# Block-causal attention and FFN on one core: softmax normalisation of the first two batches on POOL instead of DVE

## The chip, the cores and the metric

The kernel runs on one core of one Trainium2 chip. The metric is the device time of one execution in microseconds (us). Five engines work side by side, each in the order of its own instruction stream: TensorE (PE, with its weight loads PEld), VectorE (DVE), ScalarE (ACT), GpSimd (POOL) and SyncE (SP), which issues the DMA transfers here.

## What is computed

Eight batches of eight heads, 576 positions, head size 64, in fp32. The attention is causal by blocks of 64 positions; its output, the heads side by side, goes through a feed-forward network (FFN) of 512 to 2048 to 512 with a clipped-square activation.

```python
scores = scale * np.matmul(q, k.transpose(0, 1, 3, 2))
scores = np.where(block_i >= block_j, scores, -1e9)
attn = np.exp(scores - np.max(scores, axis=-1, keepdims=True))
attn = attn / (np.sum(attn, axis=-1, keepdims=True) + 1e-09)
x = np.matmul(attn, v)            # -> [4608, 512], heads side by side
h = x @ w_in
g = np.where(h >= 1, h, np.where(h <= -1, 0.0, (h + 1) ** 2 / 4))
out = g @ w_out
```

## The kernel before, in words

**Pairs and steps.** Two heads of one batch form a `Pair`; there are 32, four to a batch. `attention_steps` (L552) cuts each pair into eight steps. Each step gives PE some new work of the pair and some finishing work of an earlier step: `scores` makes one group of score tiles, and `turn` transposes the probabilities of the group scored two steps earlier. Per pair there are six groups (two heads times 128+256, 384 and 512 columns; the first holds two tiles) and one last tile of 576 columns for both heads (`scores_last`).

**One group.** PE multiplies q by k into PSUM (L371, L374), DVE takes the row maximum (L394), ACT exponentiates into the SBUF tile `pr` and sums the row into `sm` (L398), DVE adds a small constant and inverts the sum (L380, L381), and then DVE multiplies `pr` in place by this [128, 1] column (L404; L430 for the last tile). These products are the "norms" below: eight of L404 and one of L430 per pair, 3136 columns in all. After its norm, `pr` is read by PE's transposes (L443 in batches 0 to 2; from batch 3, `HOP`, a DMA copies it first and L441 reads the copy). There are three `pr` buffers.

**Weights.** The inputs of the FFN matmuls are split in a high and a low part (fp32r). `convert` (L151) makes these parts of the FFN weights in 64 pieces of 128x256, in a ring over the engines: ACT scales the two halves of the 64-bit input words (L164, L165), DVE clips, shifts and merges bits (L166, L169, L172), POOL adds integers (L178), ACT rounds to the high part (L180) and POOL subtracts for the low part (L182). The pieces are handed out over the attention steps and lie in the first quarter of the run.

**FFN.** From step 36 (`START`, in the fifth pair) each attention step also brings a half step of the FFN: 12 matmuls of L626, the activation (ACT L635, DVE L636 and L639, ACT L640, POOL L641 for the low part `gl`), and the 12 matmuls of L650 and L655. After the last pair the FFN runs alone.

**Order.** The steps are written in this order, and a scheduler of the framework then sets each engine's stream, so that the place of an instruction can differ by some rows from the written order. Also on POOL: the subtraction that splits k (L302), the split of v (L317, from batch 1) and the low part of x (L546). In batch 0 (`plain`) v and the probabilities stay unsplit.

Of the kernel before, what the change touches and what calls it, by code (L numbers as in the profile page):

```python
# [23 lines left out]
def block_attn_then_ffn(  # L24
# [9 lines left out]
    nc = tc.nc  # L34
# [42 lines left out]
    def work_bank(name):  # L77

        banks["n"] += 1
        if banks["free"] and banks["n"] % 2:  # L80
            return ps_o.tile([P, 512], F32, tag="po", name=name)
        return ps_w.tile([P, 512], F32, tag="work", name=name)
# [138 lines left out]
    def as_float32r(src):  # L221

        moved = []
        for c0 in range(0, src.shape[1], TCH):
            n = min(TCH, src.shape[1] - c0)
            pool, tag = ((conv, "bits"), (conv2, "work"))[c0 > 0]
            dst = pool.tile([P, TCH], F32R, tag=tag, name="prr")
            nc.sync.dma_start(dst[:, :n].bitcast(F32), src[:, c0 : c0 + n])
            moved.append(dst)
        return moved  # L230


    class Pair:
# [4 lines left out]
        def __init__(self, b, hp):  # L238
            self.b, self.hp = b, hp

            self.plain = b == 0
            self.first = b == 0 and hp == 0

            self.hop = b >= HOP
            self.pr, self.nat = {}, {}
# [137 lines left out]
        def scores(self, j, g):  # L383
            tiles = self.GROUPS[g]
            m = len(tiles)
            ps = work_bank("ps_s")
            pr = att3.tile([P, S], F32, tag="pr", name="pr")
            nm = small.tile([P, 2], F32, tag="nm", name="nm")
            sm = small.tile([P, 2], F32, tag="sm", name="sm")
            cols = [slice(at, at + (t + 1) * P) for t, at in tiles]  # L390
            for (t, _), cs in zip(tiles, cols):
                self.product(ps[:, cs], j, t * P, 0, (t + 1) * P, True, True)
            for i, cs in enumerate(cols):
                nc.vector.tensor_reduce(  # L394
                    out=nm[:, i : i + 1], in_=ps[:, cs], axis=AX.X, op=ALU.max, negate=True
                )
            for i, cs in enumerate(cols):
                nc.scalar.activation(  # L398
                    pr[:, cs], ps[:, cs], AF.Exp, bias=nm[:, i : i + 1], scale=1.0,
                    accum_out=sm[:, i : i + 1],  # L400
                )
            self.inverse(sm[:, :m])
            for i, cs in enumerate(cols):
                nc.vector.tensor_scalar_mul(pr[:, cs], pr[:, cs], sm[:, i : i + 1])  # L404
            self.pr[j, g] = as_float32r(pr[:, : cols[-1].stop]) if self.hop else [pr]

        def scores_last(self):

            half = S // 2
            pr = att3.tile([P, S], F32, tag="pr", name="pr")  # L410
            nm = small.tile([P, 3], F32, tag="nm", name="nm")
            sm = small.tile([P, 3], F32, tag="sm", name="sm")
            banks = []
            for i in range(2):
                ps = work_bank("ps_s")
                for j in range(2):
                    self.product(ps[:, :half], j, SM, i * half, half, j == 0, j == 1)
                nc.vector.tensor_reduce(
                    out=nm[:, i : i + 1], in_=ps[:, :half], axis=AX.X, op=ALU.max, negate=True
                )  # L420
                banks.append(ps)
            nc.vector.tensor_tensor(out=nm[:, 2:3], in0=nm[:, 0:1], in1=nm[:, 1:2], op=ALU.min)
            for i in range(2):
                nc.scalar.activation(
                    pr[:, i * half : (i + 1) * half], banks[i][:, :half], AF.Exp,
                    bias=nm[:, 2:3], scale=1.0, accum_out=sm[:, i : i + 1],
                )
            nc.vector.tensor_tensor(out=sm[:, 2:3], in0=sm[:, 0:1], in1=sm[:, 1:2], op=ALU.add)
            self.inverse(sm[:, 2:3])
            nc.vector.tensor_scalar_mul(pr, pr, sm[:, 2:3])  # L430
            self.pr["last"] = as_float32r(pr) if self.hop else [pr]

        def split(self, ps, hi, lo=None):
# [307 lines left out]
```

## Time and profile before

| | |
|---|---|
| median of 3 runs | 1284.82 us (1283.32 to 1285.23) |
| the profiled execution's own time | 1285.23 us |
| its span, first to last instruction | 1283.5 us |
| mean granted TensorE clock | 0.983 |
| busy share PE / DVE / ACT / POOL | 94% / 69% / 60% / 37% |
| first norms of pairs 0, 4, 7, 8 (start) | 18.1, 108.0, 245.7, 285.2 us |
| last weight piece on DVE (start of the last L172) | 253.5 us |

The profile's first part gives the busy time of each engine, the second cuts the span in 40 slices of 32 us and prints the busy share of each in tenths. Tables by stretch list, for each engine, busy time and the number of instructions in brackets. Groups list line, engine, operation, output and input, shapes, count, busy time, mean ns of one, and the engine's idle time ahead of them with what ended it. The chain of waits follows the work that ended last backwards, from each instruction to what released it. A line number is that of the kernel before; the changed kernel is two lines longer from `Pair` on.

### The profile page before, as it was taken

How to read it: one execution, taken by the hardware profiler on the slowest of the kernel's cores; microseconds unless marked ns; L12 is line 12 of the kernel's file. 1: busy time of each engine (PE TensorE's matmuls, PEld its weight loads, DVE VectorE, ACT ScalarE, POOL GpSimd, SP SyncE). 2: the span in 40 equal slices, each digit the busy share in tenths (PEclk: the TensorE clock that was granted, in tenths of full speed). 3: DMA queues.
4: the chain of work that ended last, by engine and by line, in shares of the span. 5: the costliest groups of instructions: out<-in, count | busy, mean ns of one | idle time of the engine just before them, and what ended most of it. 6: DMA issues, size and time to landing. Idle time of an engine off the chain costs nothing.

```text
span 1283.5 us, 20410 instructions
## 1 busy us (share of the span) xinstructions
PE 1207.2 (94%) x6496; PEld 1018.7 (79%) x6496; DVE 888.4 (69%) x2204; ACT 766.3 (60%) x1855; POOL 472.2 (37%) x466
## 2 busy tenths in 40 slices
PE   5877787899999999999999999999999999999998
PEld 4666665688888888888888888888888888888886
DVE  8998999877677777677777777777777767322222
ACT  6878676666666666666666666666666655322222
POOL 3545766633333333333333333333333332222222
PEclk9889999999999999999999999999999999999999
DMA  5656555434333545555444644464545443333432
GB/s 152 175 151 180 170 186 177 145 125 140 97 106 111 189 143 153 160 159 178 147 155 154 187 137 152 153 189 148 159 146 186 156 142 120 115 99 99 132 99 99
DMA packets 136812, 188.44 MB, mean 147 GB/s; under 512 B 61040, under 2 KB 87664, under 8 KB 136704
## 3 DMA queue, kind: packets, MB, share of 16 engines
q1 hardware_dynamic: 136704, 187.13, 47.2%
q8 instruction: 52, 0.85, 0.3%
q14 instruction: 56, 0.46, 0.1%
HBM read 120.59 MB, written 17.83 MB: 108 GB/s over the span
## 4 chain that ended last, share of the span: by engine, by line
PE 70%; DVE 13%; ACT 8%; issue 4%; DMA 2%; POOL 1%; SPq 1%; ACTq 0%; POOLq 0%; DVEq 0%
PE ph L626 26%; PE po L650 16%; PE po L655 8%; PE ps_av L480 7%; PE ps_s L371 3%; PE ps_s L374 3%; ACT pr L398 3%; PE ps_t L441 3%; PE ps_qk L327 2%; DVE pr L404 2%; ACT qb L331 2%; DVE nm L394 2%; DVE work L169 1%; PE ps_t L443 1%; DVE work L172 1%
## 5 line engine op out<-in xcount | busy, mean ns | idle before, releaser
L641 POOL TENSOR_TENSOR gl<-t,gh 128x512 fp32r<-128x512 f32 x144 | 187.2, 1300 | 577.5 <-ACT gh L640 310.8
L650 PE MATMUL po<-wo,gh 128*128 128x512 f32 x1152 | 299.7, 403 | 0.1
L650 PEld LDWEIGHTS po<-wo,gh 128*128 128x128 f32 x1152 | 210.6, 190 | 40.3 <-ACT gh L640 0.6
L626 PE MATMUL ph<-xh,wih 128*128 128x512 f32 x576 | 238.2, 414 | 1.7 <-DVE t L639 1.7
L636 DVE SCALAR_TENSOR_TENSOR t<-t 128x512 f32<-128x512 f32 x144 | 112.9, 784 | 183.1 <-ACT t L635 181.0
L626 PE MATMUL ph<-xl,wih 128*128 128x512 f32 x576 | 227.4, 395 | 1.1 <-DVE xl L516 1.1
L626 PE MATMUL ph<-xh,wil 128*128 128x512 f32 x576 | 227.9, 396 | 0.0
L635 ACT ACTIVATE t<-ph 128x512 f32<-128x512 f32 x144 | 86.0, 597 | 155.2 <-PE ph L626 155.2
L398 ACT ACTIVATE pr<-ps_s,nm 128x128 f32<-128x128 f32 (+3 forms) x256 | 134.2, 529 | 63.1 <-DVE nm L394 62.8
L655 PE MATMUL po<-wo,gl 128*128 128x512 f32 x576 | 155.4, 391 | 0.0
L394 DVE TENSOR_REDUCE nm<-ps_s 128x1 f32<-128x128 f32 (+3 forms) x256 | 123.6, 485 | 45.2 <-PE ps_s L374 43.6
L371 PE MATMUL ps_s<-ka,qa 68*128 68x288 f32 (+4 forms) x384 | 123.6, 336 | 20.5 <-ACT pr L398 12.8
L640 ACT CAST gh<-t 128x512 fp32r<-128x512 f32 x144 | 90.0, 625 | 84.6 <-DVE t L639 83.0
L626 PEld LDWEIGHTS ph<-xh,wil 128*128 128x128 f32 x576 | 109.4, 190 | 24.5
L434 ACT CAST pb<-ps_t 128x512 fp32r<-128x512 f32 (+1 forms) x140 | 77.5, 553 | 84.8 <-PE ps_t L441 65.5
L317 POOL TENSOR_TENSOR vsr<-vn,vsr 128x256 fp32r<-128x256 f32 (+1 forms) x112 | 82.9, 750 | 119.9 <-ACT vsr L316 119.9
L655 PEld LDWEIGHTS po<-wo,gl 128*128 128x128 f32 x576 | 108.4, 188 | 23.4
L626 PEld LDWEIGHTS ph<-xl,wih 128*128 128x128 f32 x576 | 109.9, 191 | 20.4 <-DVE xl L516 1.4
L626 PEld LDWEIGHTS ph<-xh,wih 128*128 128x128 f32 x576 | 109.4, 190 | 20.3 <-DVE t L639 2.0
L374 PE MATMUL ps_s<-kb,qb 128*128 128x288 f32 (+4 forms) x384 | 121.8, 323 | 0.0
L436 DVE TENSOR_TENSOR pb<-ps_t,pb 128x512 fp32r<-128x512 f32 (+1 forms) x140 | 88.1, 629 | 40.5 <-ACT pb L434 40.5
L404 DVE TENSOR_SCALAR pr<-pr,sm 128x128 f32<-128x128 f32 (+3 forms) x256 | 110.3, 451 | 3.6
(95 smaller groups left out, 2039.1 us busy)
## 6 DMA issues: line engine op xcount, KB each, us to landing
wo<-wo_split SPq DMA_DIRECT2D x144, 512.0 KB, 3.4
prr<-pr SPq DMA_DIRECT2D x80, 192.0 KB, 2.6
prr<-pr SPq DMA_DIRECT2D x60, 256.0 KB, 2.4
out_dram<-ob SPq DMA_DIRECT2D x36, 256.0 KB, 4.0
qn<-in_q_dram SPq DMA_DIRECT2D x32, 256.0 KB, 2.9
kn<-in_k_dram SPq DMA_DIRECT2D x32, 256.0 KB, 3.0
bits<-in_moe_w_in_dram SPq DMA_DIRECT2D x32, 256.0 KB, 3.1
bits<-in_moe_w_out_dram SPq DMA_DIRECT2D x32, 256.0 KB, 3.1
```

The source lines that it names most:

```text
L371: nc.tensor.matmul(ps, qa[:KA, j, c0 : c0 + P], ka[:KA, j, k0 : k0 + n], start=first, stop=False)
L374: nc.tensor.matmul(ps, qb[:, j, c0 : c0 + P], kb[:, j, k0 : k0 + n], start=False, stop=last)
L394: nc.vector.tensor_reduce(out=nm[:, i : i + 1], in_=ps[:, cs], axis=AX.X, op=ALU.max, negate=True)
L398: nc.scalar.activation(pr[:, cs], ps[:, cs], AF.Exp, bias=nm[:, i : i + 1], scale=1.0, accum_out=sm[:, i : i + 1],)
L404: nc.vector.tensor_scalar_mul(pr[:, cs], pr[:, cs], sm[:, i : i + 1])
L480: nc.tensor.matmul(ps[:, lo_col:], vt, x, start=first and i == 0 and m == 0, stop=last and i == len(parts) - 1 and m == len(mov) - 1,)
L626: nc.tensor.matmul(ph, w[:, cc, fs], x[:, cc, xs], start=(cc == 0 and i == 0), stop=(cc == NCC - 1 and i == 2),)
L636: nc.vector.scalar_tensor_tensor(out=t_, in0=t_, scalar=1.0, in1=t_, op0=ALU.min, op1=ALU.mult)
L640: nc.scalar.copy(gh, t_)
L641: nc.gpsimd.tensor_tensor(out=gl, in0=t_, in1=gh.bitcast(F32), op=ALU.subtract)
L650: nc.tensor.matmul(po[tt], gh[:, ts_], wo[:, w, :], start=(fc == 0 and w == 0), stop=False)
L655: nc.tensor.matmul(po[tt], gl[:, ts_], wo[:, 0, :], start=False, stop=fc == NFC - 1)
```

## The change

A field of `Pair` names the engine of the norms: POOL for batches 0 and 1 (the first eight pairs), DVE for all others. All 72 norms of these eight pairs (64 of L404 and 8 of L430) change engine; nothing else is written differently.

```diff
             self.plain = b == 0
+
+            self.norm = nc.gpsimd if b < 2 else nc.vector
             self.first = b == 0 and hp == 0
...
             self.inverse(sm[:, :m])
             for i, cs in enumerate(cols):
-                nc.vector.tensor_scalar_mul(pr[:, cs], pr[:, cs], sm[:, i : i + 1])
+                self.norm.tensor_scalar_mul(pr[:, cs], pr[:, cs], sm[:, i : i + 1])
...
             self.inverse(sm[:, 2:3])
-            nc.vector.tensor_scalar_mul(pr, pr, sm[:, 2:3])
+            self.norm.tensor_scalar_mul(pr, pr, sm[:, 2:3])
```

The scheduler places the moved instructions and shifts some neighbours. On DVE, in the second pair (batch 0), between the inversion of the first group's sums and the casts that follow, before the change:

```order
L381 RECIPROCAL sm<-sm 128x2
L291 TENSOR_SCALAR qs<-qn 128x64
L172 SCALAR_TENSOR_TENSOR work<-work 128x256
L404 TENSOR_SCALAR pr<-pr,sm 128x128
L404 TENSOR_SCALAR pr<-pr,sm 128x256
L380 TENSOR_SCALAR sm<-sm 128x1
L351 CAST qa<-ps_qk 64x2x64
L381 RECIPROCAL sm<-sm 128x1
L166 TENSOR_SCALAR work<-work 128x256
L404 TENSOR_SCALAR pr<-pr,sm 128x384
L351 CAST ka<-ps_qk 64x2x64
L169 TENSOR_SCALAR work<-work 128x256
```

The same place on DVE after the change (L383 is the former L381, L294 the former L292, L303 the former L301):

```order
L383 RECIPROCAL sm<-sm 128x2
L293 TENSOR_SCALAR qs<-qn 128x64
L172 SCALAR_TENSOR_TENSOR work<-work 128x256
L294 SCALAR_TENSOR_TENSOR qs<-qn,qs 128x9x64
L382 TENSOR_SCALAR sm<-sm 128x1
L353 CAST qa<-ps_qk 64x2x64
L383 RECIPROCAL sm<-sm 128x1
L166 TENSOR_SCALAR work<-work 128x256
L303 CAST ks<-kn 128x8x64
L353 CAST ka<-ps_qk 64x2x64
L169 TENSOR_SCALAR work<-work 128x256
L303 CAST ks<-kn 128x64
```

The norms are gone, and the splits of the next pair's q and k move up into their places.

On POOL in the fifth pair, the first of batch 1, around the split of the next pair's k (L302), before the change:

```order
L182 TENSOR_TENSOR ws<-work,ws 128x256
L178 TENSOR_TENSOR work<-work,bits 128x256
L182 TENSOR_TENSOR wil<-work,wih 128x256
L178 TENSOR_TENSOR work<-work,bits 128x256
L302 TENSOR_TENSOR ks<-kn,ks 128x9x64
L182 TENSOR_TENSOR wil<-work,wih 128x256
L178 TENSOR_TENSOR work<-work,bits 128x256
L641 TENSOR_TENSOR gl<-t,gh 128x512
```

The same place on POOL after the change (L304 is the former L302, L406 and L432 the norms, L643 the former L641):

```order
L182 TENSOR_TENSOR ws<-work,ws 128x256
L304 TENSOR_TENSOR ks<-kn,ks 128x9x64
L178 TENSOR_TENSOR work<-work,bits 128x256
L182 TENSOR_TENSOR wil<-work,wih 128x256
L406 TENSOR_SCALAR pr<-pr,sm 128x512
L178 TENSOR_TENSOR work<-work,bits 128x256
L432 TENSOR_SCALAR pr<-pr,sm 128x576
L182 TENSOR_TENSOR wil<-work,wih 128x256
L406 TENSOR_SCALAR pr<-pr,sm 128x128
L406 TENSOR_SCALAR pr<-pr,sm 128x256
L178 TENSOR_TENSOR work<-work,bits 128x256
L406 TENSOR_SCALAR pr<-pr,sm 128x384
```

Five norms now stand between the weight pieces' integer adds (L178), each of which waits for ACT and DVE, and the FFN's `gl` (L643) follows behind all of them. On PE the order differs in a few places of the first 800 of its some 6400 matmuls and not behind them; DVE's and ACT's orders agree again from the ninth pair on.

## The prediction

> **What bounds the kernel now.** I read the page first: its engine totals, its 40 slices, then a table of the stretches in which the eight pairs lie.
>
> ```profile
> PE 1207.2 (94%) x6496; PEld 1018.7 (79%) x6496; DVE 888.4 (69%) x2204; ACT 766.3 (60%) x1855; POOL 472.2 (37%) x466
> PE   5877787899999999999999999999999999999998
> DVE  8998999877677777677777777777777767322222
> POOL 3545766633333333333333333333333332222222
> ```
>
> Over the run PE is the bound, but the totals mix two stages. In the first eight slices (to about 257 us) DVE shows 8 and 9 and PE 5 to 8; from the ninth on PE stands at 9. The norms that move lie in the first stage, from 18.1 us to about 275 us.
>
> ```profile
> core 0: us, PE busy (x) PEld busy (x) DVE busy (x) ACT busy (x) POOL busy (x), PEclk, DMA share, GB/s
> 18.00:108.00 90.00, 71.36 (x376) 56.84 (x376) 81.07 (x242) 75.45 (x215) 47.43 (x61) 0.91 0.57 165
> 108.00:147.00 39.00, 29.83 (x160) 23.71 (x159) 36.31 (x91) 29.71 (x81) 25.02 (x29) 0.96 0.58 174
> 147.00:246.00 99.00, 77.83 (x376) 62.63 (x375) 89.91 (x202) 66.30 (x176) 62.95 (x71) 0.91 0.55 175
> 246.00:285.00 39.00, 34.82 (x188) 29.70 (x187) 29.82 (x69) 23.61 (x59) 16.06 (x17) 0.96 0.40 125
> 285.00:319.00 34.00, 34.00 (x193) 29.34 (x193) 25.14 (x65) 22.45 (x54) 11.62 (x10) 1.00 0.44 135
> ```
>
> The cuts are first norms: 18 to 108 us are pairs 0 to 3 (attention and weight pieces), 108 to 147 pair 4, 147 to 246 pairs 5 and 6 (with FFN and weight pieces), 246 to 285 pair 7, and 285 to 319 is the first pair of the steady stage, where PE is busy all the time. DVE is busy 90%, 93% and 91% of the first three stretches: it is the bound there. In the fourth PE is at 89% and DVE at 76%, so no gain is to be had from DVE there. Behind 285 us nothing changes but the start: what is won or lost ahead of it passes one for one into the time.
>
> The chain of waits says the same of the stretch from 18 to 147 us, and less of 147 to 285 us:
>
> ```profile
> by line: issue 9.9%; DVE pr L404 9.4%; DVE work L166 8.7%; DVE nm L394 6.3%; DVE work L169 6.1%; DVE work L172 5.9%; PE ps_t L443 4.6%; ACT kb L331 4.3%; POOL work L178 3.0%; ACT pr L398 2.9%; ACT work L164 2.4%; ACT pb L434 2.3%; DMA bits<
> by line: issue 9.2%; DVE work L169 7.8%; PE ph L626 7.6%; DVE work L172 6.5%; POOL work L178 4.7%; ACT pr L398 4.1%; DVE pr L404 4.0%; DVE t L636 3.6%; DVE nm L394 3.6%; DVE work L166 3.4%; ACT work L164 2.9%; ACT qb L331 2.9%; PE po L650 2
> ```
>
> L404 carries 9.4% of 129 us and 4.0% of 138 us: 12.1 + 5.5 = 17.6 us of the chain.
>
> **What goes from DVE.** The same stretches for L404 and for L430 alone:
>
> ```profile
> 18.00:108.00 90.00, 19.69 (x32) 0.91 0.57 165
> 108.00:147.00 39.00, 5.42 (x8) 0.96 0.58 174
> 147.00:246.00 99.00, 11.16 (x18) 0.91 0.55 175
> ```
>
> ```profile
> 18.00:108.00 90.00, 2.03 (x4) 0.91 0.57 165
> 108.00:147.00 39.00, 0.52 (x1) 0.96 0.58 174
> 147.00:246.00 99.00, 1.18 (x2) 0.91 0.55 175
> ```
>
> So DVE loses 21.7, 5.9 and 12.3 us of busy time in the first three stretches. Much of that is waiting: from 18 to 285 us (the first four rows) a norm takes up to 1.8 times what it takes from 300 to 1100 us (the other four):
>
> ```profile
> L404 DVE TENSOR_SCALAR pr<-pr,sm 128x512 f32<-128x512 f32 x16 | 13.5, 841 | 0.2
> L404 DVE TENSOR_SCALAR pr<-pr,sm 128x384 f32<-128x384 f32 x16 | 12.2, 762 | 0.1
> L404 DVE TENSOR_SCALAR pr<-pr,sm 128x256 f32<-128x256 f32 x16 | 8.7, 542 | 0.0
> L404 DVE TENSOR_SCALAR pr<-pr,sm 128x128 f32<-128x128 f32 x16 | 7.5, 466 | 0.1
> ```
>
> ```profile
> L404 DVE TENSOR_SCALAR pr<-pr,sm 128x512 f32<-128x512 f32 x47 | 22.5, 478 | 0.8
> L404 DVE TENSOR_SCALAR pr<-pr,sm 128x384 f32<-128x384 f32 x47 | 20.0, 425 | 0.9
> L404 DVE TENSOR_SCALAR pr<-pr,sm 128x256 f32<-128x256 f32 x47 | 16.3, 347 | 0.0
> L404 DVE TENSOR_SCALAR pr<-pr,sm 128x128 f32<-128x128 f32 x47 | 13.4, 285 | 1.4
> ```
>
> What they wait for is seen in the time line: at 218.6 us L172 starts under a POOL instruction that began 0.06 us earlier, and ends 0.28 us after it, with 1.50 us in place of its median of 0.416.
>
> ```profile
> 218.54 1.28 POOL L641 TENSOR_TENSOR gl<-t,gh 128x512 fp32r<-128x512 f32 x1 [3.15 <-ACT gh L640]
> 218.60 1.50 DVE L172 SCALAR_TENSOR_TENSOR work<-work 128x256 uint32<-128x256 uint32 x1
> ```
>
> The three DVE lines of the weight pieces, with minimum, median and maximum over the run, and with their means from 18 to 285 us:
>
> ```profile
> L169 DVE TENSOR_SCALAR work<-work x64: 267/291/1534, 10.7 to 251.7; 128x256 uint32<-128x256 uint32 x64
> L172 DVE SCALAR_TENSOR_TENSOR work<-work x64: 397/416/1631, 13.3 to 253.5; 128x256 uint32<-128x256 uint32 x64
> L172 DVE SCALAR_TENSOR_TENSOR work<-work 128x256 uint32<-128x256 uint32 x63 | 36.6, 583 | 0.6
> L169 DVE TENSOR_SCALAR work<-work 128x256 uint32<-128x256 uint32 x62 | 31.6, 516 | 0.5
> L166 DVE TENSOR_SCALAR work<-work 128x256 f32<-128x256 f32 x62 | 27.2, 442 | 6.8 <-ACT work L164 6.7
> ```
>
> **What comes to POOL.** POOL runs no such product now, so its cost is bounded by neighbours: the one-input selects on POOL, its two-input subtraction, and below by DVE's own.
>
> ```profile
> L123 POOL TENSOR_SCALAR_AFFINE_SELECT msel<-msel 4x256 f32<-4x256 f32 x1 | 0.4, 411 | 3.0 <-DVE qs L291 3.0
> masks.py:199 POOL TENSOR_SCALAR_AFFINE_SELECT ident_f<-ident_f 128x128 f32<-128x128 f32 x1 | 0.3, 292 | 0.0
> L641 POOL TENSOR_TENSOR gl<-t,gh 128x512 fp32r<-128x512 f32 x95 | 122.7, 1292 | 416.3 <-ACT gh L640 154.4 <-ACT vsr L316 137.3 <-issue 123.7
> L178 POOL TENSOR_TENSOR work<-work,bits x64: 729/748/1616, 14.3 to 254.0; 128x256 int32<-128x256 int32 x64
> ```
>
> The selects give (411 - 292)/128 = 0.93 ns a column and 0.17 us for each: 0.65 us for 512 columns, and for the 3136 columns and nine norms of a pair 2.9 + 1.5 = 4.5 us, 36 us in eight pairs. The two-input rows give (1292 - 729)/256 = 2.2 ns a column, 8.4 us a pair and 67 us in all. DVE's own (3.1 us for the eight of a pair at the undisturbed times, and 0.5 for the last) is 3.6 us, 28 us in all; I see no reason for POOL to be quicker. I take 36, since a norm has one tensor input as the selects have, and keep 28 and 67. The GPSIMD Engine Reference of the Trainium skill, section 4.1, calls one-input work on POOL roughly line-rate and two-input work about twice as slow as DVE; by that the sum is that of the selects, and no row here shows it for a product.
>
> **The sum.** POOL's busy time from 18 to 285 us is 47 + 25 + 63 + 16 = 151 us, so 36 us more is +24%. The three DVE lines of the weight pieces wait about 63 x 0.17 + 62 x 0.22 + 62 x 0.15 = 34 us for POOL (mean less median, L166 against the median of L169, an operation of its size); I let that grow by the same quarter, 9 us, split 3, 1.5 and 4.5.
> - 18 to 108: DVE 81.1 - 21.7 + 3 = 62. Now ACT, at 75.5, is the fullest. If ACT gets as full as DVE did, 90%, the stretch takes 84 us: -6.2.
> - 108 to 147: DVE 36.3 - 5.9 + 1.5 = 32, at 90% 35.5: -3.5.
> - 147 to 246: DVE 89.9 - 12.3 + 4.5 = 82, at 91% 90.4: -8.6. PE (78) and POOL (63 + 10 for 20 norms) lie below.
> - 246 to 285: PE's stretch, nothing.
>
> That is -18, close to the 17.6 us of L404 in the chain. Against it stands the hand-over. A norm on DVE followed its inversion on the same engine; on POOL it stands in line with L178 and L182, and those wait:
>
> ```profile
> L178 POOL TENSOR_TENSOR work<-work,bits 128x256 int32<-128x256 int32 x62 | 51.2, 829 | 64.3 <-ACT bits L165 12.4 <-DVE sm L381 10.2 <-DVE work L172 9.3
>   DVE pr L404: 6.0, 10
> ```
>
> POOL stands idle for 64.3 us ahead of 62 adds, 1.0 us each; a norm behind such an add is late by that, and PE's transposes with it, and behind these on PE the next scores. PE has waited for a norm ten times so far (second row, of L443), for 6.0 us. The two steps between `scores` and `turn` are 5 to 6 us in the first stretch and 12 in the third, which hides most; I charge ten exposed turns at 0.8 us, the wait and a norm 0.17 us longer less what DVE's shorter line brings forward: +8. The cover is that lag: without it the 40 turns of the eight pairs would all be late. The `gl` of the FFN (L641) also stands behind norms, and the transposes of the third stretch with it; that is in the same charge.
>
> -18 + 8 = -10 us against the profiled execution's 1285.2 (span 1283.5; its time lies 0.4 above the median of the three runs): **1275 us**.
>
> **The rivals.**
> - *The whole DVE gain comes through.* The lag hides the hand-over, as it does for all but ten turns now, and only the -18 stays, or a little more where DVE no longer holds POOL up: 1264 to 1268. Against it: POOL's 64 us of waiting, which the norms inherit.
> - *The path that POOL and DVE exclude each other from is the bound.* L172's 1.50 us shows that some of their instructions do not overlap. A norm takes that path on either engine, on POOL 36 us in place of DVE's 28. Then nothing of the 40 us that leave DVE is won but what was waiting, and this comes back at L166, L169 and L172; the 8 us more are paid where the path is fullest, or hidden: 1281 to 1293, about 1286. For it: 34 us of waits on three lines. Against it: DVE's row maxima (L394) and PSUM work don't wait so, and in the first stretch DVE loses 24% of its time. The Trainium skill (SBUF — State Buffer, section "SBUF: two separate sides") describes this as an exclusive lock on a shared port pair, held for a whole instruction, and its Perfetto Trace Analysis, "Optimizing Scalar/DVE Operations", says that offloading between these two might therefore not help. The trace agrees with the lock (1.50 against 0.416 us); on the outcome no run here speaks yet.
> - *Slower: POOL's line makes the turns late.* At the two-input rate a norm of 512 columns takes 1.29 us, 0.81 more than DVE's, and POOL would be busy 47 + 4 x 8.4 = 81 of the first 90 us, as full as DVE is now, waits not counted. If all 40 turns are late by 0.8 us, that is +32 against -18: +14, 1299. It decides from 18/40 = 0.45 us of exposed delay per turn. For it: POOL's waits of 1.0 us ahead of its adds. Against it: the lag of two steps.
>
> **How the numbers follow.** Forecast (about 1269 to 1281) 0.42; the whole gain 0.16; the shared path 0.20; POOL's line 0.22. The range goes from 1262 to 1297: under it lies a larger gain than worked out here, above it the worse half of the last rival. Measurement tells 0.2%, 2.6 us, from no change. Faster by more: forecast and whole gain, 0.58, and a little of the shared path, 0.59. Same: the middle of the shared path, 0.11. Slower: its rest and POOL's line, 0.30.
>
> **What would show it.** In the changed kernel the first norm back on DVE (pair 8, now at 285.2 us) should stand near 275, and the steady stage behind it as long as before. DVE should be near 75% in 18 to 100 us with ACT above it, POOL's norm of 512 columns near 0.65 to 0.75 us, L166, L169 and L172 some 0.05 us longer in the mean, and PE's waits for a norm near 14 us in place of 6.0. A norm of 512 columns over 1 us, or PE waits for norms above 25 us, would make it wrong; so would a first stretch that is no shorter though DVE is emptier.

## The result, and the profile after

The changed kernel took **1319.96 us** (median of 4 runs, 1318.2 to 1322.52), the kernel before 1285.03 us (4 runs): a ratio of 1.0265 with a 95% interval of 1.0238 to 1.0292. It is slower by 35 us, on the other side from the forecast of 1275 us and 23 us above the end of the range.

The page of the changed kernel, engine totals and four rows of its 40 slices (now 32.9 us each):

```profile
PE 1219.1 (93%) x6496; PEld 1027.7 (78%) x6496; DVE 860.7 (65%) x2132; ACT 766.3 (58%) x1855; POOL 552.9 (42%) x538
PE   4777678689999999999999999999999999999998
DVE  6665777876777777767777777777777777322222
POOL 5878777775333333323333333333333332222221
PEclk9878788889999999999999999999999999999999
```

DVE did become emptier (5 to 8 in place of 8 and 9), and POOL went from 3 to 7 up to 5 to 8. No engine stands at 9 in the first eight slices, and yet they last longer: a stage in which nobody is full is a stage of waits. POOL has 80.7 us more busy time, where 36 were charged (the norms add more than that, and its other instructions got a little shorter: L178 went from 833 to 781 ns in the mean).

The table by stretch, cut where the norms of pairs 0, 4, 5, 7 and 8 begin, with the columns of the one above:

```profile
18.00:124.00 106.00, 77.93 (x380) 60.81 (x381) 65.99 (x207) 74.11 (x212) 87.26 (x92) 0.82 0.48 135
124.00:170.00 46.00, 32.33 (x154) 25.82 (x153) 32.39 (x81) 30.82 (x83) 36.60 (x42) 0.81 0.53 159
170.00:279.00 109.00, 79.69 (x368) 64.49 (x367) 84.88 (x185) 66.46 (x177) 82.70 (x92) 0.86 0.52 161
279.00:318.00 39.00, 36.69 (x198) 30.89 (x197) 26.22 (x58) 23.54 (x59) 25.48 (x25) 0.96 0.38 118
318.00:352.00 34.00, 34.00 (x194) 29.33 (x194) 25.21 (x66) 22.48 (x54) 11.56 (x10) 1.00 0.43 135
```

DVE fell from 81.1 to 66.0 us in the first stretch and its share from 90% to 62%; the stretch grew by 16 us. The second and third grew by 7 and 10, the fourth by nothing, and the pair of the steady stage is as before. From the start of pair 8 to the end the two executions differ by 0.1 us (1001.5 and 1001.6): the whole loss lies in pairs 0 to 6.

For the experiments I use a sharper cut, the starts of the first row maximum of pairs 0, 4, 5, 7 and 8 in the one profiled execution of each kernel:

| us | pairs 0-3 | pair 4 | pairs 5-6 | pair 7 | sum |
|---|---|---|---|---|---|
| before | 88.7 | 38.3 | 98.8 | 41.4 | 267.2 |
| change | 104.4 | 44.5 | 110.4 | 40.8 | 300.2 |

What a norm takes on POOL, by groups of line and shape up to 320 us (count, busy time, mean ns, idle time before):

```profile
L406 POOL TENSOR_SCALAR pr<-pr,sm 128x512 f32<-128x512 f32 x16 | 26.2, 1636 | 7.0 <-DVE sm L383 6.4 <-ACT work L164 0.5
L406 POOL TENSOR_SCALAR pr<-pr,sm 128x384 f32<-128x384 f32 x16 | 21.7, 1359 | 1.2 <-DVE sm L383 0.7 <-DMA wo<-wo_split 0.5
L406 POOL TENSOR_SCALAR pr<-pr,sm 128x256 f32<-128x256 f32 x16 | 16.7, 1043 | 0.0
L432 POOL TENSOR_SCALAR pr<-pr,sm 128x576 f32<-128x576 f32 x8 | 13.8, 1729 | 2.4 <-ACT pr L400 2.0 <-DVE sm L383 0.4
L406 POOL TENSOR_SCALAR pr<-pr,sm 128x128 f32<-128x128 f32 x16 | 12.9, 806 | 5.7 <-DVE sm L383 3.4 <-PE ps_t L445 1.2 <-DVE sm L382 0.7
```

Together 91.3 us, 2.5 times the 36 charged and above the upper bound of 67. Undisturbed norms take 0.60 us for 128 columns and 1.56 for 512, which is 2.5 ns a column and 0.28 us each.

Who waits for POOL now, by the view of waits up to 310 us (total, times, longest):

```profile
ACT wih L180 <- POOL work L178: 38.5, 20, 5.7
PEld ps_t L445 <- POOL pr L406: 35.0, 25, 6.4
PE ps_t L445 <- POOL pr L406: 26.5, 20, 5.9
DVE work L166 <- ACT work L164: 25.5, 19, 3.1
ACT ws L180 <- POOL work L178: 12.1, 7, 3.8
ACT work L164 <- POOL ws L182: 8.6, 7, 2.8
```

The same view of the kernel before, up to 250 us:

```profile
ACT wih L180 <- POOL work L178: 15.4, 18, 2.3
ACT ws L180 <- POOL work L178: 4.8, 6, 1.9
PEld ps_t L443 <- DVE pr L404: 4.1, 6, 1.1
ACT work L164 <- POOL ws L182: 5.6, 6, 3.0
```

Three waits for POOL stand out. PE's turns wait for the norms (L445). ACT's rounding of the weight pieces waits for POOL's integer add (L180 for L178), and everything behind it in ACT's stream with it. DVE's clip L166 now waits 25.5 us for ACT's scaling, where it waited 6.7; this wait stays (28.8 us) in the kernel further below in which ACT no longer waits for the add, so that the add is not its only cause. And ACT's first scaling (L164) waits until POOL's subtraction (L182) has released a `work` buffer. Over all lines ACT waits 61.3 us for POOL up to pair 8, by a sum over the trace, where it was 25.9.

The list of what PE waits for ahead of L445 adds the two sides of TensorE, weight load and matmul, so that one late turn can count twice; before it was 6.0 us:

```profile
  POOL pr L406: 61.4, 45
  POOL pr L432: 18.6, 8
```

One late turn, with its causes, in the time line of the changed kernel:

```profile
49.41 1.41 POOL L304 TENSOR_TENSOR ks<-kn,ks 128x576 fp32r<-128x576 f32 x1
50.78 0.78 POOL L178 TENSOR_TENSOR work<-work,bits 128x256 int32<-128x256 int32 x1
51.59 0.40 ACT L180 CAST wih<-work 128x256 fp32r<-128x256 f32 x1 [3.37 <-POOL work L178]
53.50 0.15 DVE L383 RECIPROCAL sm<-sm 128x1 f32<-128x1 f32 x1
53.66 0.73 POOL L178 TENSOR_TENSOR work<-work,bits 128x256 int32<-128x256 int32 x1 [0.86 <-DVE sm L383]
54.37 1.78 POOL L406 TENSOR_SCALAR pr<-pr,sm 128x512 f32<-128x512 f32 x1
56.20 1.11 PE L445 MATMUL ps_t<-ident_r,pr 128*128 128x128 f32 x4 [4.24 <-POOL pr L406]
58.00 0.56 DVE L396 TENSOR_REDUCE nm<-ps_s 128x1 f32<-128x384 f32 x1 [1.82 <-PE ps_s L376]
```

In this stretch it reads as a circle. POOL's add at 50.78 comes late behind the split of k, ACT stands still for 3.37 us until it is there, and with ACT the exponentials and so the inversion of their sums (53.50). The norm then stands behind another add and takes 1.78 us, PE stands still for 4.24 us until 56.20, and the row maximum of a later group waits 1.82 us for PE. Each engine here is idle part of the time because another one is late by POOL.

### The profile page after: what moved, and what is told of

Read it like the earlier page. It is cut to its first block, busy times and chain, and to the rows that moved or that the text cites. A ratio compares the mean times of both kernels' runs of the same rounds, so it can differ in the third digit from the quotient of the medians.

```text
span 1316.4 us, 20474 instructions
## 1 busy us (share of the span) xinstructions
PE 1219.1 (93%) x6496; PEld 1027.7 (78%) x6496; DVE 860.7 (65%) x2132; ACT 766.3 (58%) x1855; POOL 552.9 (42%) x538
## 4 chain that ended last, share of the span: by engine, by line
PE 69%; DVE 5%; ACT 4%; issue 2%; DMA 1%; POOL 1%; ACTq 0%; POOLq 0%
PE ph L628 26%; PE po L652 16%; PE po L657 8%; PE ps_av L482 7%; PE ps_s L376 3%; PE ps_s L373 3%; PE ps_t L443 3%; PE ps_qk L329 2%; ACT pr L400 2%; ACT qb L333 1%; PE ps_t L445 1%; DVE nm L396 1%; DVE sm L382 1%; DVE pr L406 1%; DMA prr<-pr 1%
## 5 line engine op out<-in xcount | busy, mean ns | idle before, releaser
L643 POOL TENSOR_TENSOR gl<-t,gh 128x512 fp32r<-128x512 f32 x144 | 186.1, 1292 | 568.1 <-ACT gh L642 295.8
L373 PEld LDWEIGHTS ps_s<-ka,qa 68*128 68x128 f32 x384 | 76.0, 198 | 39.2 <-ACT pr L400 17.8
```

Of the source, the lines that this page charges most:

```text
L373: nc.tensor.matmul(ps, qa[:KA, j, c0 : c0 + P], ka[:KA, j, k0 : k0 + n], start=first, stop=False)
L643: nc.gpsimd.tensor_tensor(out=gl, in0=t_, in1=gh.bitcast(F32), op=ALU.subtract)
```

## The experiments

Ratios are to the kernel before, run beside it on the same chip, with 95% intervals. All edits but the last touch the first eight pairs or the weight pieces only. Times of single stages come from one profiled execution of each kernel.

### What the norm costs on POOL, and how much that matters

**A quarter of the columns**, by which a norm costs about what was assumed:

```diff
-                self.norm.tensor_scalar_mul(pr[:, cs], pr[:, cs], sm[:, i : i + 1])
+                part = slice(cs.start, cs.stop if self.b > 1 else cs.start + (cs.stop - cs.start) // 4)
+                self.norm.tensor_scalar_mul(pr[:, part], pr[:, part], sm[:, i : i + 1])
```

> The norms of the first two batches on POOL, but each over the first quarter of its columns only (the other three quarters stay unnormalised), so that a norm costs about 0.36 to 0.64 us, 4.5 us a pair: the price the prediction assumed, with the same hand-over from DVE to POOL to PE. Theory A (the price of a norm on POOL, 10.4 us a pair undisturbed, is what made the change slow): 1275 us, between 1265 and 1283. Theory B (the place in POOL's line is what costs, whatever the norm takes): still slower than before, 1300 or more. Theory C (POOL's busy time costs, through the weight pieces and DVE's waits): in proportion to it, about 1285 to 1295.

Measured 1294.86 us, 1.0076 (1.0056 to 1.0096). The group of its norms (minimum, median, maximum in ns):

```profile
L407 POOL TENSOR_SCALAR pr<-pr,sm x64: 358/598/1251, 18.1 to 286.6; 128x32 f32<-128x32 f32 x16, 128x64 f32<-128x64 f32 x16, 128x96 f32<-128x96 f32 x16, 128x128 f32<-128x128 f32 x16
```

With 45 us of norms on POOL, a quarter more than the 36 that I had put in, the kernel is still 10 us slower than before, where 10 us quicker was forecast. So a right price alone would not have made the forecast right. Of the three theories the one that goes by POOL's busy time had the range.

**The two-input form**, the same product with the column repeated as a second tensor:

```diff
+                    nc.gpsimd.tensor_tensor(out=pr[:, cs], in0=pr[:, cs],
+                        in1=sm[:, i : i + 1].to_broadcast([P, cs.stop - cs.start]), op=ALU.mult)
```

> The change with each norm on POOL written as a product of two tensors, the column repeated along the row. By the rows of before (128x512 in 1.29 us, 128x256 in 0.73 us) a norm of 512 columns takes 1.29 us in place of 1.56, 8.4 us a pair in place of 10.4. Theory A or P: the loss goes down with the price, by about 16 us x (0.27 + 0.2) = 7 us, to 1312 us. If the column read costs (one scalar for each partition), not the product, the time per norm falls further, below 1 us, and the loss by half, 1300 us.

Measured 1302.01 us, 1.0126 (1.0106 to 1.0146). Its group of 512 columns:

```profile
L407 POOL TENSOR_TENSOR pr<-pr,sm 128x512 f32<-128x512 f32 x16 | 16.8, 1049 | 5.2 <-DVE sm L383 1.9 <-ACT bits L165 1.5 <-PE ps_av L488 1.2
```

The form with two tensors is the quicker one on POOL, 1.05 us against 1.64, all norms together 60.7 us, and the kernel gains 18 us on the change for 31 us less on POOL. The price is a large part of the loss, and not all. The time came out near the 1300 us of the second case, though a norm did not fall below 1 us as that case had it.

**A constant in place of the column** (the division by the sum is left out):

```diff
-                self.norm.tensor_scalar_mul(pr[:, cs], pr[:, cs], sm[:, i : i + 1])
+                self.norm.tensor_scalar_mul(pr[:, cs], pr[:, cs], 1.0 if self.b < 2 else sm[:, i : i + 1])
```

> The change with a constant in place of the column of sums (no normalisation in the first two batches): the same one-input product on POOL without a scalar read for each partition. If the column costs, 512 columns take 0.65 us as the selects' rate had it, and the time is near 1295 us; if the product as such is slow on POOL, 1.5 us as before, and 1315 to 1320 us.

Measured 1300.09 us in a single run (before: 1285.58), so without an interval.

```profile
L406 POOL TENSOR_SCALAR pr<-pr 128x512 f32<-128x512 f32 x16 | 24.5, 1531 | 9.3 <-ACT pr L400 6.0 <-PE ps_t L445 3.2
```

The price hardly fell (1.53 us; 84 us in all), and yet the kernel is some 20 us quicker than the change, between the two times expected. Such a norm need not wait for DVE's inversion: it starts right after the exponential, and PE's waits for norms, both sides, fall from 80 to 42 us. So it seems to count when the norm may start, and not only how long it takes.

### What DVE's relief is worth

**No norms at all in the first two batches** (the division is left out):

```diff
+                if self.b > 1:
                     self.norm.tensor_scalar_mul(pr[:, cs], pr[:, cs], sm[:, i : i + 1])
```

> The norms of the first two batches are left out on every engine. This shows what an emptier DVE gives at most: by the prediction's sum -18 us, 1267 us. If another limit stands right behind DVE (ACT's line, PE's latency, the shared path), 1278 us or more. Theories A, B and C don't differ here.

Measured 1274.52 us, 0.9921 (0.9904 to 0.9938). This is the most that taking them off DVE can bring with all else as it is: 10.4 us and not 18. By stage it is 4.9 us in pairs 0 to 3 (6.2 predicted), a loss of 1.0 in pair 4 (a gain of 3.5 predicted), 1.7 in pairs 5 and 6 (8.6 predicted) and 4.9 in pair 7 (nothing predicted). Where the time stays in pairs 5 and 6 is seen in its stretch:

```profile
138.00:235.00 97.00, 80.14 (x377) 65.09 (x377) 79.83 (x182) 67.49 (x178) 63.63 (x74) 0.89 0.57 179
```

DVE and PE are both at 80 of 97 us; with the norms gone nobody is full, and the stretch is hardly shorter. DVE at 91% had not been the only thing that held its pace.

### The load on POOL without the hand-over

**DVE keeps its norms, and POOL makes a product of the same size that nobody reads:**

```diff
                 nc.vector.tensor_scalar_mul(pr[:, cs], pr[:, cs], sm[:, i : i + 1])
+                if self.b < 2:
+                    nc.gpsimd.tensor_scalar_mul(xl[:, :n, 2 * S : 2 * S + P],
+                        ident.unsqueeze(1).to_broadcast([P, n, P]), sm[:, i : i + 1])
```

> The kernel before, norms on DVE, and in addition POOL makes a product of the same size after each inversion (the last one over 512 in place of 576 columns), from a constant tile into columns that nothing reads: POOL's load of the change without anyone waiting for a norm. Theory A with late turns as its way: DVE waits more for POOL, but no turn is late: 1288 to 1300 us. Theory C (load alone, by way of the weight pieces and the waits of DVE): the whole loss and more, since DVE keeps its norms: 1320 us or more. Theory B (place in line of the norms): within 5 us of before.

Measured 1310.71 us, 1.0200 (1.0183 to 1.0217), with 95.4 us of such products on POOL.

**The same, with DVE's norms left out** (the division is left out):

```diff
-                nc.vector.tensor_scalar_mul(pr[:, cs], pr[:, cs], sm[:, i : i + 1])
+                if self.b >= 2:
+                    nc.vector.tensor_scalar_mul(pr[:, cs], pr[:, cs], sm[:, i : i + 1])
+                else:
+                    self.idle((cs.stop - cs.start) // P, sm[:, i : i + 1])
```

Here `idle` is the unread product above.

> POOL's product of the same size from a constant tile, read by nobody, and no norms at all in the first two batches (the probabilities stay unnormalised): the engines carry the load of the change, but no turn waits for POOL. Theory P (three terms that add: relief of DVE -10, load of POOL +26, late turns the remaining +19): 1285 - 10 + 26 = 1301 us. Theory Q (no term of its own for late turns; POOL's line is simply the bound, and it is as full here): 1315 to 1322 us, as the change.

Measured 1312.65 us, 1.0209 (1.0192 to 1.0226). No turn waits for a norm on POOL in either, and three quarters of the loss are there. Neither time lies where an expectation had it: the first is between those of two theories, the second between P's 1301 us and Q's 1315. Nor does it matter whether DVE does its norms: with POOL loaded, no gain from the relief of DVE can be measured. In the second kernel's waits the weight pieces stand first:

```profile
ACT wih L180 <- POOL work L178: 38.4, 22, 4.3
DVE work L166 <- ACT work L164: 25.2, 15, 3.5
```

This wait of ACT for POOL's add is what it was in the change (38.5); in the first of the two kernels it is 28.5 us.

### One wait at a time

**Only the last tile's norms on POOL** (8 of 72):

```diff
-            nc.vector.tensor_scalar_mul(pr, pr, sm[:, 2:3])
+            (nc.gpsimd if self.b < 2 else nc.vector).tensor_scalar_mul(pr, pr, sm[:, 2:3])
```

> Only the norm of the last tile of each pair (576 columns, eight in all, 1.72 us each on POOL) goes to POOL, the other 64 stay on DVE. Theory A: DVE loses 4.2 us, POOL gains 14 us, one turn of five per pair is about 1.2 us later: within 4 us of before, 1283 to 1289. Theory B: each of eight hand-overs costs about what one of 40 costs in the change, 35/40 = 0.9 us: 1290 to 1293. Theory C: 14 of 91 us of load, +5: 1290.

Measured 1292.66 us, 1.0063 (1.0047 to 1.008). Eight norms, some 14 us of POOL time at the durations above, cost 8 us. Pairs 0 to 3 grow by 5.6 us. (The expectation counts five turns in a pair; `attention_steps` has seven, six groups and the last tile.)

**One step more between POOL's add and ACT's rounding**, in the change and in the kernel before:

```diff
         nc.gpsimd.tensor_tensor(out=w32, in0=w32, in1=low, op=ALU.add)
         w32 = w32.bitcast(F32)
+        yield
         nc.scalar.copy(hi(), w32)
...
-    LAG = 2
+    LAG = 3
```

> The changed kernel, with one more step between POOL's integer add of a weight piece (L178) and ACT's rounding of its result (L180), so that ACT has a step in hand where it now waits for POOL. If the load of POOL costs by way of ACT's waits for that add (20 us before, 51 us after): 1300 to 1310 us. If it costs by DVE's waits on the shared path or the late turns alone: within 5 us of the change, 1315 to 1325 us.

> The kernel before with the extra step between L178 and L180, the twin of e11. If the step costs nothing by itself: 1283 to 1288 us, and e11 says that it doesn't help the change. If the longer hold of the three weight buffers costs: 1292 us or more, and e11's 1324 us holds a gain that this cost hides.

Measured 1324.48 us, 1.0302 (1.0281 to 1.0322), and 1291.62 us, 1.0047 (1.0032 to 1.0062). The edit itself costs 6 us, and the change costs 33 us on top of it, much as it does without. More distance did not help. This settles nothing on which wait it is, since a piece that takes a step more also holds its `work` buffer for longer.

**ACT's rounding doesn't wait for POOL's add** (it rounds DVE's clipped value, which leaves POOL's sum out of the high part), in the change and in the kernel before:

```diff
-        nc.scalar.copy(hi(), w32)
+        nc.scalar.copy(hi(), top)
```

> The changed kernel, but ACT's rounding of a weight piece (L180) reads DVE's clipped value in place of POOL's sum (so the weight parts are wrong): POOL does all it does in the change, and ACT never waits for POOL's add. Theory R (POOL's load costs by ACT's stream standing behind that add): against its twin on the kernel before (the next run) the change costs the late turns and little more, +5 to +18 us. Rival S (POOL's line itself, or DVE's waits for POOL, sets the pace): still +30 us or more against the twin.

> The twin of the run ahead: the kernel before, with the same freeing of ACT from POOL's add. ACT waits 26 us for POOL there until the ninth pair, so at most that is to be won, and DVE is full: 1275 to 1286 us under both theories.

Measured 1318.29 us, 1.0254 (1.0231 to 1.0277), and 1288.58 us, 1.0021 (1.001 to 1.0032): the change still costs 30 us. So ACT's wait alone does not make the loss. The twin is 3 us slower than before, above its expected range; why stays open. The turns wait on, as in the change:

```profile
PEld ps_t L445 <- POOL pr L406: 32.0, 24, 5.4
PE ps_t L445 <- POOL pr L406: 23.8, 18, 4.9
PE ps_t L445 <- POOL pr L432: 14.4, 5, 4.1
```

### All ways but one

At this point taking away the turns' waits alone had brought 7 us of the 35, and taking away ACT's wait alone 2 (5 against its twin). Either the load itself was the cause, or several waits hold the same pace, so that taking one leaves the others. The next four kernels take them away together.

**POOL loaded, no norms, and ACT doesn't wait for the add** (the two edits above together; left out are the division and, in the high part, POOL's sum):

> POOL's product of the same size read by nobody, no norms in the first two batches, and ACT's rounding of the weight pieces fed by DVE's clipped value: POOL is as loaded as in the change, but neither PE's turns nor ACT's stream wait for its norms or its adds. If these two waits are the ways of the loss, each enough by itself: near e2, 1275 to 1290 us. If a third way is (DVE's waits for POOL, the split of k, gl): 1305 us or more.

Measured 1298.45 us, 1.0102 (1.0079 to 1.0124). Pairs 0 to 3 fall from 100.0 to 86.9 us, pairs 5 and 6 stay at 108.6 (110.0). The time lies between the two expected ranges. The waits for POOL that are left in pairs 5 and 6, from 146 to 254.7 us:

```profile
ACT work L164 <- POOL wil L182: 7.7, 4, 3.7
ACT work L164 <- POOL ws L182: 6.7, 4, 2.7
```

ACT's next piece waits for a `work` buffer that POOL's subtraction frees.

**The same, and POOL's two operations of a weight piece work on other operands**, so that they hold no `work` buffer (the low parts of the weights are left out):

```diff
-        nc.gpsimd.tensor_tensor(out=w32, in0=w32, in1=low, op=ALU.add)
+        nc.gpsimd.tensor_tensor(out=low, in0=low, in1=low, op=ALU.add)
...
-        nc.gpsimd.tensor_tensor(out=lo(), in0=w32, in1=hi().bitcast(F32), op=ALU.subtract)
+        nc.gpsimd.tensor_tensor(out=lo(), in0=hi().bitcast(F32), in1=hi().bitcast(F32), op=ALU.subtract)
```

> As e20 (POOL's load of the change, no turn and no rounding waits for POOL), and in addition POOL's two instructions of a weight piece keep their size but no longer read or write the buffer that ACT fills next (the add stays inside the input words, the subtraction reads the high part twice, so the low parts are zero). If the hold of that buffer is the third way: pairs 5 and 6 fall from 109 us to about 99, and the time from 1298 to 1285 to 1290 us. If DVE's waits for POOL or POOL's other work are: within 4 us of e20, 1295 to 1302 us.

Measured 1279.74 us, 0.9945 (0.9925 to 0.9966): quicker than before, and than the 1285 to 1290 us expected. Its stretch up to pair 8 shows how busy POOL still is:

```profile
14.80:275.00 260.20, 214.74 (x1071) 172.64 (x1070) 219.41 (x534) 193.78 (x530) 216.71 (x248) 0.88 0.55 170
```

POOL is busy 216.7 of 260.2 us, 83%, the share of DVE (84%), and the kernel is 5 us above the one without norms and without load (in which the pieces still wait). A loaded POOL costs little here when hardly anything waits for it. The load is not quite the same, though: on their new operands L178 and L182 are shorter, 87 us together where the kernel ahead has 101, so that the gain on it, some 20 us, is that of the free buffers and of a load some 14 us lighter.

**The change with its norms, and the weight pieces freed from POOL in the same way** (POOL's sum and the low parts of the weights are left out), and **the kernel before with the same edit:**

> The change, with the norms on POOL as they are there, but with the weight pieces freed from POOL: ACT rounds DVE's clipped value, and POOL's L178 and L182 work on other operands, so that nobody waits for the add and no `work` buffer waits for POOL (the low parts of the weights are wrong). Theory T (PE's turns that wait for the norms hold the pace of pairs 0 to 3 by themselves; the weight pieces matter in pairs 5 and 6 only): 1296 to 1308 us, pairs 0 to 3 still over 98 us and PE's waits for norms over 50 us, pairs 5 and 6 at 97 to 101. Theory W (the turns wait because POOL's line is held up by its own waits for ACT and DVE; once its adds are free, the norms come in time): under 1290 us, PE's waits for norms under 30 us.

> The kernel before with the same freeing of the weight pieces from POOL; the norms stay on DVE (the low parts of the weights are wrong). It is the twin of the other run of this call, and the base for the run in which POOL carried the load and nobody waited for it. If POOL's part in the weight pieces holds up the kernel before as well, 1268 to 1278 us; if DVE is its only bound, 1282 to 1287 us.

Measured 1303.76 us, 1.0150 (1.0132 to 1.0169), and 1274.55 us, 0.9918 (0.9896 to 0.9939). The first theory of the expectation holds by each of its numbers: PE's waits for norms, both sides of TensorE added, are 84 us:

```profile
  POOL pr L406: 58.1, 39
  POOL pr L432: 26.2, 9
```

Pairs 0 to 3 take 102.5 us and pairs 5 and 6 99.6. The norms are late even when the adds ahead of them wait for nobody but ACT's L165. POOL's part in the weight pieces also held up the kernel before, by some 10 us.

The kernels in one table, ratio to before and, behind it, pairs 0 to 3 and pairs 5 and 6 in us:

| | weight pieces wait for POOL | they don't |
|---|---|---|
| norms on DVE | 1; 88.7; 98.8 | 0.9918; 89.4; 95.2 |
| norms on POOL, turns wait | 1.0265; 104.4; 110.4 | 1.0150; 102.5; 99.6 |
| same load on POOL, no norms, no turn waits | 1.0209; 100.0; 110.0 | 0.9945; 82.1; 98.9 |
| neither load nor norms | 0.9921; 83.9; 97.1 | not run |

Down the right column, the turns' waits alone are 1.0150 - 0.9945 = 2.05%, 26 us. Along the third row, the weight pieces' waits alone are 2.64%, 34 us: 14 of them come with ACT's wait for the add, at the same load, and the rest with the `work` buffers and the lighter load of the right column. Both together are 3.2%, 41 us, and not 60: in pairs 0 to 3 one of them is enough for 100 us, and the second adds 2 to 4. In pairs 5 and 6 only the weight pieces count (110 against 99): the two steps between `scores` and `turn` are twice as long there, and the trace of the change has no wait of PE for a norm in them (60 us in pairs 0 to 3, 20 in pair 4, both sides). That is why undoing one wait at a time showed so little.

### The other direction

**POOL's subtraction L182 goes to DVE**, in the kernel before and in the change:

```diff
-        nc.gpsimd.tensor_tensor(out=lo(), in0=w32, in1=hi().bitcast(F32), op=ALU.subtract)
+        nc.vector.tensor_tensor(out=lo(), in0=w32, in1=hi().bitcast(F32), op=ALU.subtract)
```

> The kernel before with the opposite move: the subtraction that makes the low part of a weight piece (L182, 64 times, 51 us on POOL) goes from POOL to DVE, where it takes some 0.42 us undisturbed (27 us). Theory P with its rates (0.27 us per us of POOL's load, 0.23 per us of DVE's): -14 + 6 to 8, 1278 us. If DVE is the bound as the prediction had it (90% busy): +27 and its waits, 1300 us or more.

> The changed kernel with L182, 51 us of POOL's work, moved to DVE, which has room since the norms left: both waits stay, but POOL's line has 182 us of work until the ninth pair in place of 232. If the fullness of POOL's line is the cause: most of the loss goes, 1285 to 1298 us. If the hand-over of a norm costs by itself: 1310 us or more (the change less the 5 us that this move is worth on the kernel before).

Measured 1280.57 us, 0.9953 (0.9935 to 0.9971), and 1307.47 us, 1.0175 (1.0156 to 1.0194). Work added to the engine that seemed to be the bound makes the kernel quicker:

```profile
L182 DVE TENSOR_TENSOR wil<-work,wih 128x256 fp32r<-128x256 f32 x32 | 18.7, 585 | 0.9 <-ACT wih L180 0.8
L182 DVE TENSOR_TENSOR ws<-work,ws 128x256 fp32r<-128x256 f32 x32 | 18.2, 570 | 1.9 <-ACT ws L180 1.9
L169 DVE TENSOR_SCALAR work<-work 128x256 uint32<-128x256 uint32 x64 | 20.4, 324 | 0.2
```

DVE takes on 36.9 us, and gets part of it back as L169 falls from 516 to 324 ns with fewer POOL instructions beside it. With the change on top it is some 28 us slower again, between the two cases expected: relieving POOL of the 64 subtractions is not enough for the turns, and PE's waits for norms, both sides, are still 66 us.

**The same, without the addition of 1e-9** (each sum is at least 1, so that fp32 rounds it away):

```diff
-            nc.vector.tensor_scalar_add(total, total, EPS)
```

> The kernel before with L182 on DVE (1280.6 us in its own run, -5.5) and, in all batches, without the addition of 1e-9 to the row sums (L380), which are at least 1, so that fp32 drops it anyway: DVE loses 51 small instructions of 0.145 us until the ninth pair. By the rate of e2 (10 us for 45 us of DVE) another -2: 1278 us. If DVE isn't what is short there: 1280 to 1281.

Measured 1273.22 us, 0.9906 (0.9886 to 0.9926). This version beats both kernels, by 12 us and 47 us. The addition's part is 6 us by the ratios, where 2 were expected; why stays open.

## Why the prediction was wrong, point by point

**"36 us more is +24%" on POOL: the price failed.** I read the cost per column from two selects of 128 and 256 columns, on 128 and on 4 partitions, and took two-input rows for the upper bound. Measured are 91.3 us, +60%, 10.4 us a pair undisturbed in place of 4.5. A product with a column of scalars costs 2.5 ns a column here, more than the subtraction with two tensors. The upper bound was none, since nothing made the scalar form cheaper than the rows that I had. Of the rule named in the prediction, that one-input work on POOL is roughly line-rate and two-input work slower (the Trainium skill, GPSIMD Engine Reference, section 4.1), the traces show the opposite order for this operation: for 512 columns 1.05 us with two tensors and 1.64 with one tensor and a column, against 0.48 on DVE with the column.

**"I charge ten exposed turns at 0.8 us": the step that decided.** This +8 was the whole price of the hand-over in the sum; in its place the two waits for POOL together measure 41 us, by the table. It was the wrong size and one half of the mechanism. The ten were waits on two sides of TensorE; the six of the weight-load side were the turns. In the change 25 waits for L406 stand on that side, 1.4 us each, the longest 6.4 us. With the weight pieces out of the way the turns' waits cost 26 us. The lag of two steps, named as the cover, does hide them in pairs 5 and 6, and not in pairs 0 to 4. The count was wrong as well: a pair has seven turns and not five, 56 in the eight pairs in place of 40.

**What was not in the sum at all.** I asked who waits for the norms, and, but for the FFN's `gl`, not who waits for what stands behind them on POOL. L178 and L182 stand behind norms; ACT waits for the one (50.6 us in the change, 20.2 before), the `work` buffers for the other. This alone is up to 34 us, at the loads of the table's third row.

**"That is -18": the relief was little more than half as large.** At most 10.4 us could be had, and nearly half of it lies in pair 7, where nothing was forecast. The step "If ACT gets as full as DVE did, 90%" lets another engine fill up to the same share; in pairs 5 and 6 DVE fell to 82% with the norms gone, PE, the fullest, stood at 83%, and the stretch fell to 97.1 us only. The weight pieces' waits for POOL may have held it there in part (freeing them in the kernel before gave 3.6 us, taking the norms away 1.7). The 17.6 us of L404 in the chain of waits agreed with the sum, but a chain's share is what an instruction takes and not what the kernel gains without it.

**"I let that grow by the same quarter, 9 us": it did not.** L166, L169 and L172 stood at 442, 516 and 583 ns up to pair 8, 95.4 us together; after the change they take 96.9 us:

```profile
L172 DVE SCALAR_TENSOR_TENSOR work<-work 128x256 uint32<-128x256 uint32 x63 | 37.0, 589 | 0.7
L169 DVE TENSOR_SCALAR work<-work 128x256 uint32<-128x256 uint32 x62 | 30.9, 502 | 0.6
L166 DVE TENSOR_SCALAR work<-work 128x256 f32<-128x256 f32 x62 | 29.0, 473 | 23.2 <-ACT work L164 23.1
```

For all DVE instructions that overlap with POOL up to pair 8, I estimate from the traces some 62 us above the times of the same instructions without overlap before, and some 53 after. The rival of the shared path was right that DVE and POOL hinder each other, and wrong on the outcome: in the kernel where POOL is loaded and hardly anything waits for it the same estimate is 65 us, the highest of the three, and it is quicker than before. So the sentence that offloading between these two might not help (the Trainium skill, Perfetto Trace Analysis, "Optimizing Scalar/DVE Operations") holds here in its outcome, but these figures do not show the port that it names as the reason.

**The rival that was right in its place.** "POOL's line makes the turns late" named the wait, the condition (0.45 us of exposed delay per turn) and the side. Its price (+14) took 0.8 us a turn from the two-input rate, counted 40 turns where there are 56 (with them 18 us of relief are 0.32 us a turn), and left out the weight pieces.

**What was right.** All is decided ahead of pair 8, and the steady stage moved by 0.1 us. Each of the three signs that I had named as making the forecast wrong was there: a norm of 512 columns at 1.64 us (over 1), the turns' row at 80 us (over 25), a first stretch longer with DVE emptier. The first norm back on DVE stands at 318.1 us, not near 275.

**What stays open.** Pair 4 takes 41 to 46 us in every kernel with the full load, also when hardly anything waits for POOL (44.4), and 36 to 41 without. In the kernel with these 44.4 us TensorE's granted clock in pair 4 is 0.77, where it was 0.96 before, and PE is busy 34.1 us there in place of 29.7; whether the clock, the waits of DVE for POOL or POOL's load makes pair 4 longer was not told apart. The kernel without load and with the weight pieces free was not run, so the load's own cost is known only as 5 us against a base in which the pieces still wait. The edit that frees the `work` buffers also spares POOL's add its wait for DVE, besides making POOL's instructions shorter. What part of the loss is TensorE's lower clock (below) was not separated from the waits: up to pair 8 PE is busy 226.2 us for 1086 matmuls in the change and 213.4 us for as many before, so that by this it is at most 13 of the 33 us. The kernel in which hardly anything waits for POOL has 216.7 us, and a clock of 0.88 against 0.92, and is quicker than before all the same.

## What to carry to other kernels

Before work goes to an engine that looks idle, list what stands behind it in that engine's stream and who waits for each of these, results and buffers alike; a share of 50% says nothing of lateness in a line that is served in order. Price the operation in its exact form (engine, kind of operands, width) or take a bound that no form can exceed. When undoing one suspect at a time brings little, undo all and put them back one by one: waits that hold the same pace hide each other.

## What the runs showed of the hardware

- On POOL the product with a column of scalars is slower than the product with that column repeated as a second tensor: 1.64 us against 1.05 in the mean for 512 columns. With a constant it takes 1.53, so that the reading of the column is a small part of it at most.
- The granted clock of TensorE was lower in the three stretches in which PE waited more than before, 0.82, 0.81 and 0.86 against 0.91, 0.96 and 0.91, and 1.00 where PE is always busy.
